# A fused adaLN, local-attention and gated-MLP kernel on one core: the opening's loads on two queues, another order of the work behind it, an edge constant built on GpSimd, and the gate row in column tiles

## The chip, the core and the metric

The kernel runs on one NeuronCore of a Trainium2 chip. A core has a matrix engine (TensorE, PE in the profile, with its weight loads shown apart as PEld), three engines for everything else (VectorE or DVE, ScalarE or ACT, GpSimd or POOL) and SyncE (SP), which issues transfers. Transfers issued by SP run on the queue q1 of the profile, those of GpSimd on q0, those of ScalarE on q10; all share the core's 16 DMA engines. The metric is the device time of one execution in microseconds. Three executions of the kernel before took 544.57, 543.80 and 543.88 us, median 543.88 us.

## The reference

One transformer block with 2048 rows and 576 columns, conditioned on one vector `c`.

```
mod = (silu(c) @ w_mod).reshape(1, 6, 1, 576)      # sa, ca, ga, sb, cb, gb
h = layernorm(x) * (1 + ca) + sa
q, k, v = h @ wqkv                                 # 32 heads of 18
logits[s, w] = q[s] . k[s - 2 w] * 18 ** -0.5      # w = 0..7, masked before row 0
x = x + ga * ((softmax(logits) @ v[s - 2 w]) @ wo)
h = layernorm(x) * (1 + cb) + sb
x = x + gb * (((h @ w_gate) * (h @ w_up)) @ w_down)   # 576 -> 4608 -> 576
```

Inputs and output are bfloat16. `sa`, `ca`, `sb`, `cb` act on columns of `h`, which stand on partitions in the kernel's transposed `h`. The two gates `ga` and `gb` act on rows of 576 columns and are therefore needed as one row repeated on all 128 partitions.

## The kernel before

The 2048 rows are eight chunks of 256 (`CH`), each of two tiles of 128 rows (`j` = 0, 1). The chunks go through attention one after the other and through the MLP in five groups, `[0], [1, 2], [3, 4], [5, 6], [7]`. The schedule is written out by hand: every engine does its instructions in the order of the program, a transfer is asked for by the engine that names it, and a later instruction of that engine waits behind it.

**Opening, 0 to 20 us.** SP asks for chunk 0 of x in two pieces (L203), the last 64 rows of the first two blocks of `w_mod` (`load_wm_tail`, two transfers, L190), the other 512 rows (L206), then `wqk`, chunk 1 of x, more of `wqk`, `wv` and `wmC` (the block of `ga`). ScalarE asks for `c` in three pieces into five partitions (L185, L187). PE turns `c` by one transpose (L1029); `keep_busy` (L199) gives it dummy matmuls meanwhile. `mod_columns` (L321 to L347) multiplies silu(c), repeated over 32 columns, with `wmA` in four column tiles at once, `k` order `KF, 0, 1, 2, 3`; the result is evicted to `mrow`, transposed, and added into `modc`. The normed chunk 0 is transposed in between (`x0_ts`) and evicted through `modc` to `hT`. Only then can the first matmul of q (L416) run. GpSimd meanwhile makes constants, among them `edge`.

**Middle, 20 to 48.8 us.** Chunk 0's attention by halves `j`: `pj` (products of q with a shifted k, DVE), `lj` (their head sums, PE), `max_j` and `sum_j` (softmax, DVE with an exponential on ACT), `shift_attn` (PE), `av_mul` (DVE), `av_sum` (PE), `b_wj` (the product with `wo`, PE, then the gated residual on DVE). Between them stand chunk 1's q, k, v (`a_q`, `a_v`) and chunk 2's norm. The first 16 rows of the second tile reach back into the first tile; they are corrected by `edge_mul` (DVE) and five matmuls with `edge_t`, which PE makes by seven matmuls from `edge` (L1143) and ACT copies. `mod_row` (L349) makes `ga` for all partitions: ten matmuls of full width with 512 and 64 columns, copied to `ga_bc`.

**Groups.** `gate_up` runs 36 steps `f`; each is a pair of 64-row matmuls for gate and up (L706). Four steps share one block of weights, 0.5 MB for gate and 0.5 MB for up, loaded by SP (`load_wgu`). Block 3 of group 0 has no buffer of its own: it stands in the tile `hh` (`wgu_home[3]`, L1319). Small pieces of other work stand between the steps. A planner (`timed`, L808) places them at build time: each piece is a tuple (PE cost, DVE cost, marks it needs, mark it sets, delay until that mark holds, call). In group 0 one thread of pieces loads the block of `gb` on GpSimd's queue (`load_wm5`) and, 12 planner units later, runs `gb_row` (L1257): `mod_row` for `gb`, then `ld_d1(3)`, a load of 576 KB of `w_down` on GpSimd's queue into a part of `hh` that nothing uses yet. Another thread is chunk 3's norm, made on ACT in two pieces of two instructions each (`norm_of`, L683).

Of the kernel before, what the change touches and what calls it, by code (L numbers as in the profile page):

```python
# [7 lines left out]
BF = mybir.dt.bfloat16  # L8
# [17 lines left out]
W = 8  # L26
# [12 lines left out]
VR = H - VA  # L39

# [4 lines left out]
def kernel(  # L45
# [31 lines left out]
    vstage = pool("vstage", 2)  # L77
# [25 lines left out]
    ga_bc = consts.tile([P, D], F32, name="ga_bc")  # L103
    gb_bc = consts.tile([P, D], F32, name="gb_bc")
# [10 lines left out]
    vd = dramp.tile([HALO + S, D], BF, name="vd")  # L115
    prod_t = consts.tile([P, 4 * KT * CH], BF, name="prod_t")
# [67 lines left out]
    c_row = sp.tile([KT, P], BF, name="c_row")  # L184
    nc.scalar.dma_start(c_row[0:KF, :], c[0, 0:KF * P].rearrange("(m p) -> m p", p=P))  # L185
    for c0 in (0, 64):
        nc.scalar.dma_start(c_row[KF:KT, c0:c0 + 64], c[:, KF * P:D])  # L187
    def load_wm_tail(wm, blk):
        for b in range(2):
            nc.sync.dma_start(wm[64 * b:64 * (b + 1), KF, b * D:(b + 1) * D], w_mod[KF * P:D, (blk + b) * D:(blk + b + 1) * D])  # L190
# [11 lines left out]
    for j in range(ST):  # L202
        nc.sync.dma_start(x_in[0][:, j, :], x_flat[js(j), :])  # L203
    load_wm_tail(wmA, 0)
# [23 lines left out]
    for k in range(2):  # L228
# [11 lines left out]
    edge = sp.tile([HALO, W - 1, P], BF, name="edge")  # L240
    edge_t = sp.tile([P, HALO], BF, name="edge_t")
# [3 lines left out]
    nc.gpsimd.affine_select(out=edge[:], in_=edge[:], compare_op=ALU.not_equal, fill=1.0, base=-2,  # L245
                            pattern=[[-(HALO + DIL), W - 1], [1, P]], channel_multiplier=-1)
    nc.gpsimd.affine_select(out=edge[:], in_=edge[:], compare_op=ALU.is_ge, fill=0.0, base=SPAN - 1,
                            pattern=[[-DIL, W - 1], [0, P]], channel_multiplier=-1)
    nc.gpsimd.memset(wo[64:, KF, :], 0.0)
# [10 lines left out]
    def ln_parts(src, tag, act=False, both=None):  # L260
# [22 lines left out]
        def norm_act(j):  # L283
            nb = small.tile([P, 1], F32, name="ln_nb")
            nc.vector.scalar_tensor_tensor(nb[:], mv[:, j, 0:1], -1.0, rstd[:, j:j + 1], ALU.mult, ALU.mult)
            for d0, s0, n in ((0, 0, D), (D, D - 64, 64))[0:2 if both else 1]:
                nc.scalar.activation(xn[:, j, d0:d0 + n], src(j)[:, s0:s0 + n], ACTF.Identity, bias=nb[:], scale=rstd[:, j:j + 1])
        return xn, stat, rsq, (norm, norm_act) if act is None else norm if not act else norm_act

    def layernorm(src, tag, act=False, both=None):  # L290
        xn, stat, rsq, norm = ln_parts(src, tag, act, both)
        for j in range(ST):
            stat(j)

        def norms(js=range(ST)):
            for j in js:
                norm(j)
        return xn, lambda: rsq(slice(0, ST)), norms
# [22 lines left out]
    def mod_columns(wm, pi, fill=lambda: None, steps={}):  # L321
        pm = ps([P, 320], F32, "pm")
        order = (KF, 0, 1, 2, 3)
# [25 lines left out]
    def mod_row(wm, dst):  # L349
        pa = ps([P, 512], F32, "pa")  # L350
        pb = ps([P, 64], F32, "pb")
        for p_t, c0, c1 in ((pa, 0, 512), (pb, 512, D)):
            for kt in range(KT):
                m = wm(kt)
                rows = slice(0, m.shape[0])
                nc.tensor.matmul(p_t[:], lhsT=sc_bc[rows, kt, :], rhs=m[:, c0:c1],
                                 start=(kt == 0), stop=(kt == KT - 1))
        nc.scalar.copy(dst[:, 0:512], pa[:])
        nc.scalar.copy(dst[:, 512:D], pb[:])
# [176 lines left out]
    def shift_attn(j):  # L536
# [6 lines left out]
        if j > 0:  # L543
            pzb = ps([P, H], F32, "pzb")
            for w in range(W - 1):
                nc.tensor.matmul(pzb[:], lhsT=edge[:, w, :], rhs=attn0[0:HALO, j, w, :], start=(w == 0), stop=(w == W - 2))
# [11 lines left out]
    def av_sum(j, hf, acc={}):  # L558
# [10 lines left out]
        if hf == 1:  # L569
            if j > 0:  # L570
                for d, c0 in dst:
                    nc.tensor.matmul(d[:, 0:HALO], lhsT=v_e[:].rearrange("p d h -> p (d h)")[:, c0:c0 + P], rhs=edge_t[:],
                                     start=False, stop=True, skip_group_check=True)
            nc.scalar.copy(oT[:, 0:KF, js(j)], po[:])
            nc.scalar.copy(oT[0:64, KF, js(j)], po4[64:P, :])

    def b_wj(j):
# [10 lines left out]
        def rest(stat):  # L588
            for hf, (cs, pw) in enumerate(pws):
                nc.vector.tensor_tensor(xt[:, cs], pw[:], ga_bc[:, cs], ALU.mult)  # L590
                nc.vector.tensor_tensor(xt[:, cs], xt[:, cs], x_res[0][:, j, cs], ALU.add)
                stat(j, (hf,))
        return rest
# [89 lines left out]
    def norm_of(n, after, free, load=None):  # L683
# [5 lines left out]
        norm = [(0, 0, f"r{n}", f"e{n}", 2.0, lambda: aa[n]["norm"]((0,))), (0, 0, f"e{n}", f"n{n}", 1.6, lambda: aa[n]["norm"]((1,)))]  # L689
# [325 lines left out]
    def load_wm5():  # L1015
        nc.gpsimd.dma_start(wm5(), w_mod[0:KF * P, 5 * D:6 * D].rearrange("(k p) n -> p k n", p=P))
# [11 lines left out]
    pc = ps([P, KT], BF, "pc")  # L1028
    nc.tensor.transpose(pc[:], c_row[:], ident[0:KT, 0:KT])  # L1029
    keep_busy(7, NB)  # L1030
# [25 lines left out]
    add_modc = mod_columns(wmA, 0, lambda: keep_busy(2, NB), {KF: x0_ts, 1: lambda: keep_busy(1, NB)})  # L1056
# [31 lines left out]
    ashs = {}  # L1088

    def sum_j(j):  # L1090
        ss = small.tile([P, H], F32, name="ssj")
        nc.vector.tensor_reduce(ss[:], dd0[:, j].rearrange("p w h -> p h w"), axis=AX.X, op=ALU.add)
        nc.vector.reciprocal(ss[:], ss[:])
        nc.vector.tensor_tensor(attn0[:, j], dd0[:, j], ss[:, None, :].to_broadcast([P, W, H]), ALU.mult)

    load_wm(wmC, 2, 1)
    for dd4 in range(4):
        nk = (DH - dd4 + 3) // 4
        wsrc = bass.AP(A_wo.tensor, A_wo.offset + dd4 * D, [[DH * D, H], [4 * D, nk], [1, D]])
        nc.sync.dma_start(wo[dd4 * H:(dd4 + 1) * H, 0:nk, :], wsrc)  # L1100
    load_res(0)
    load_wm_tail(wmB, 3)
    nc.sync.dma_start(wmB[:, 0:KF, :], w_mod[0:KF * P, 3 * D:5 * D].rearrange("(k p) n -> p k n", p=P))
    load_x(2)
# [36 lines left out]
    pet = ps([P, HALO], F32, "pet")  # L1141
    for w in range(W - 1):
        nc.tensor.matmul(pet[:], lhsT=edge[:, w, :], rhs=ident[0:HALO, 0:HALO], start=(w == 0), stop=(w == W - 2))  # L1143
    nc.scalar.copy(edge_t[:], pet[:])
    mod_row(lambda k: wmC[:, k, :], ga_bc)
    for w in range(4):
        lj(1, w)
    sum_j(0)
    a_q(1, 0)
    shift_attn(0)  # L1150
    for w in range(4, 8):
        pj(1, w)
    a_q(1, 1)
    for w in range(4, 8):
        lj(1, w)
    av_mul(0, 0)
    max_j(1)
    a_q(1, 2)
    av_mul(0, 1)
    sum_j(1)  # L1160
    a_q(1, 3)
    av_sum(0, 0)
    a_q(1, 4)
    av_sum(0, 1)
    shift_attn(1)
# [3 lines left out]
    xn2, stat2, rsq2, norm2 = ln_parts(lambda j: x1[0][j], "b")  # L1169
    stat2c(0)  # L1170
    stat2c(1)
    rsq2c(slice(0, 2))
    av_mul(1, 0)
    x1_halves = []

    def products_1():
        x1_halves.append(b_wj(0))
        norm2c(0)
        norm2c(1)
        a_v(1, 0)  # L1180

    add_modc = mod_columns(wmB, 1, products_1)
    x1_half = x1_halves[0]
    av_mul(1, 1)
    edge_mul()
    add_modc()
    av_sum(1, 0)
    x1_half(stat2)
    a_t(2, False)
    av_sum(1, 1)  # L1190
    b_p(1, 0)
    rsq2(slice(0, 1))
    a_v(1, 1)
# [17 lines left out]
    a_v(2, 0)  # L1211
    b_l(1, 0)
    for w in range(4, 8):
        b_p(1, w)
    a_v(2, 1)
# [41 lines left out]
    def gb_row():  # L1257
        mod_row(lambda k: wm5()[:, k, :] if k < KF else wm5r[0:64, :], gb_bc)
# [3 lines left out]
    first = [(0, 0, "", "p17", 1.4, nop), (0.75, 0, "p17", "l14", 1.0, lambda: b_l(1, 4)), (0.35, 0, "l14", "t14", 0.3, lambda: b_lt(1))] + first  # L1262
# [8 lines left out]
               [[(0, 0, "", "-", 0, lambda: (load_wm5(), load_wd(0))), (0, 0, "", "z3", 8.0, both_halves), (0, 0, "", "w5", 12.0, nop), (1.5, 0, "w5", "-", 0, gb_row), (0, 0, "", "-", 0, lambda: load_res(2))],  # L1271
# [3 lines left out]
                                         (0.6, 0.8, "n4 v3", "x4", 0, lambda: (a_t4(), load_x(6)))]]),  # L1275
# [84 lines left out]
```

## Time and profile before

| what | value |
|---|---|
| median of three runs | 543.88 us |
| the profiled execution's own time | 544.44 us |
| its span, first to last instruction | 542.7 us |
| PE busy | 535.3 us, 99% of the span |
| DVE busy, ACT busy | 58%, 46% |
| first matmul of q (L416) starts | 11.09 us |
| first matmul of gate and up (L706) starts | 48.83 us |
| DVE busy in 15 to 20, 20 to 25, 25 to 30, 30 to 35 us | 4.70, 4.81, 4.41, 4.55 of 5 us each |
| bytes moved in 48.8 to 64.6 us | 5.36 MB, 339 GB/s |
| granted TensorE clock | 1.0 |

The span is what the profile covers; the time of an execution has some 1.7 us around it. Windows of the span are given from its start. A chain of waits follows the work back from the last instruction: at each step to what released it. The DMA share is the mean busy share of the 16 engines; a little over 1 is a full engine, since records overlap.

### The profile page before, as it was taken

The page shows a single profiled execution, that of the slowest core. Times are in us where ns is not written, and L with a number is a line of the kernel's source. Part 1 is how long each engine was busy: PE and PEld are TensorE (multiplying, and loading weights), DVE is VectorE, ACT ScalarE, POOL GpSimd, SP SyncE. Part 2 cuts the span into 40 slices and gives each one's busy share as a digit, 9 for nine tenths or more (in the row PEclk, how much of TensorE's full clock was granted, in tenths as well). Part 3 has the DMA queues.
Part 4 walks back from the last instruction along what each step waited for, and adds up shares of the span by engine and source line. Part 5 has one row for each costly group of instructions (what it writes and reads, how often), then busy time and mean ns, then how long its engine had stood idle before and what let it go on. Part 6 is the DMA issues. An engine that isn't in the chain of part 4 may idle for free.

```text
span 542.7 us, 14569 instructions
## 1 busy us (share of the span) xinstructions
PE 535.3 (99%) x6157; PEld 321.9 (59%) x6189; DVE 315.9 (58%) x713; ACT 251.5 (46%) x617; POOL 67.9 (13%) x104
## 2 busy tenths in 40 slices
PE   8999999999999999999999999999999999999997
PEld 4887789756745444555544444555544445558875
DVE  4989586777766777646358896524344924032212
ACT  4776777543566553022645552014555551006630
POOL 7104012122000110111000110110010101010210
PEclk9999999999999999999999999999999999999999
DMA  8999999778872694878435983894296592849821
GB/s 264 299 261 363 336 272 332 258 224 258 267 203 89 211 208 153 227 220 293 135 108 163 232 288 68 162 239 159 89 275 176 156 311 69 255 138 294 271 74 42
DMA packets 94924, 114.52 MB, mean 211 GB/s; under 512 B 27980, under 2 KB 83676, under 8 KB 94732
## 3 DMA queue, kind: packets, MB, share of 16 engines
q1 hardware_dynamic: 83360, 67.29, 44.6%
q0 software_dynamic: 11344, 46.25, 27.8%
q8 instruction: 48, 0.79, 0.6%
q14 instruction: 16, 0.13, 0.1%
q10 hardware_dynamic: 156, 0.07, 0.0%
HBM read 103.15 MB, written 4.74 MB: 199 GB/s over the span
## 4 chain that ended last, share of the span: by engine, by line
PE 94%; DMA 3%; DVE 1%; SPq 1%; ACT 1%; issue 0%
PE pg L706 28%; PE pu L706 23%; PE acc L921 19%; PE pq L706 3%; PE accr L926 3%; PE pw L605 3%; PE pq L416 3%; PE acc L976 3%; PE lgT L470 2%; DMA wmC<-in_w_mod_dram 2%; PE pv L706 2%; PE pv L439 1%; DMA wqk<-in_A_wqkv_dram 1%; PE po L567 1%; PE pwj L584 0%
## 5 line engine op out<-in xcount | busy, mean ns | idle before, releaser
L706 PE MATMUL pg<-h2T,wgu 64*128 64x512 bf16 (+1 forms) x1376 | 265.5, 331 | 0.0
L706 PE MATMUL pu<-h2T,wgu 64*128 64x512 bf16 (+1 forms) x1376 | 264.5, 331 | 0.0
L706 PEld LDWEIGHTS <-wgu 64*128 64x128 bf16 x2752 | 136.5, 94 | 94.8 <-issue 0.5
L757 ACT CAST u_sb<-pu 128x512 bf16<-128x512 f32 (+1 forms) x172 | 85.4, 497 | 135.8 <-PE pg L706 131.2
L760 DVE TENSOR_TENSOR hh<-g_sb,u_sb 128x512 bf16<-128x512 bf16 x136 | 57.4, 423 | 116.2 <-ACT g_sb L758 115.7
L758 ACT CAST g_sb<-pg 128x512 bf16<-128x512 f32 (+1 forms) x172 | 86.7, 504 | 0.0
L921 PEld LDWEIGHTS <-hh 128*128 128x128 bf16 x504 | 49.0, 98 | 59.5 <-issue 1.5
L921 PE MATMUL acc<-wd,hh 128*128 128x512 bf16 x329 | 84.1, 380 | 0.1
L926 PE MATMUL accr<-wd,hh 128*128 128x64 bf16 x344 | 62.4, 193 | 0.7
L706 PE MATMUL pu<-h2T,wgr 64*128 64x512 bf16 (+1 forms) x188 | 61.5, 327 | 0.2 <-ACT u_sb L757 0.2
L706 PE MATMUL pg<-h2T,wgr 64*128 64x512 bf16 (+1 forms) x188 | 61.5, 327 | 0.0
L926 PEld LDWEIGHTS <-hh 128*128 128x128 bf16 x504 | 45.8, 98 | 1.9
L171 POOL DMA_DIRECT2D wd<-in_B_w_down_dram x29 | 21.8, 752 | 190.0 <-PE accr L926 93.4
L461 DVE TENSOR_TENSOR prod_t<-qT,kT 128x1280 bf16<-128x1280 bf16 x56 | 43.7, 818 | 0.7 <-ACT kT L777 0.7
L514 DVE TENSOR_TENSOR vsh<-vsh,attn 128x1152 bf16<-128x1152 bf16 x56 | 39.6, 748 | 1.2 <-DMA vsh<-vd 1.2
L706 PEld LDWEIGHTS <-wgr 64*128 64x128 bf16 x376 | 19.7, 94 | 15.4 <-issue 2.5
L921 PE MATMUL acc<-prod_t,hh 128*128 128x512 bf16 x111 | 28.8, 380 | 0.0
L304 ACT ACTIVATE h2T<-h2T,modc 128x256 bf16<-128x256 bf16 x12 | 6.6, 595 | 45.3 <-DMA h2T<-xn 45.3
L455 POOL DMA_DIRECT2D vsh<-vd x14 | 12.5, 897 | 104.8 <-DVE o_sb L524 89.6
L706 PE MATMUL pq<-hT,wqk 64*128 64x256 bf16 (+1 forms) x360 | 22.2, 259 | 0.1
L416 PE MATMUL pq<-hT,wqk 128*128 128x256 bf16 (+1 forms) x225 | 21.2, 251 | 0.4 <-ACT hT L304 0.4
L926 PE MATMUL accr<-prod_t,hh 128*128 128x64 bf16 x112 | 21.6, 193 | 0.1
(208 smaller groups left out, 605.0 us busy)
## 6 DMA issues: line engine op xcount, KB each, us to landing
wgu<-in_B_w_gate_dram SPq DMA_DIRECT2D x41, 512.0 KB, 4.5
wgu<-in_B_w_up_dram SPq DMA_DIRECT2D x41, 512.0 KB, 6.4
wd<-in_B_w_down_dram POOLq DMA_DIRECT2D x29, 576.0 KB, 5.6
vsh<-vd POOLq DMA_DIRECT2D x14, 1152.0 KB, 9.3
prod_t<-in_B_w_down_dram POOLq DMA_DIRECT2D x8, 576.0 KB, 7.6
hh<-in_B_w_down_dram POOLq DMA_DIRECT2D x6, 576.0 KB, 6.4
x_r<-in_A_x_dram SPq DMA_DIRECT2D x8, 288.0 KB, 8.3
vd<-v_sb POOLq DMA_DIRECT2D x16, 144.0 KB, 5.2
```

The lines of the kernel that those rows point to most:

```text
L171: return nc.gpsimd.dma_start(wb[:], B_w_down[r0:r0 + FB * P, :].rearrange("(k p) n -> p k n", p=P))
L416: nc.tensor.matmul(pq[:, gi, :], lhsT=wqk[:, kt, m * P:(m + 1) * P], rhs=hT[:, kt, cols], start=(kt == order[0] and not (by_k and gi)), st ...
L461: nc.vector.tensor_tensor(prod, aa[i]["qT"][:], aa[i]["kT"][:, :, off:off + CH], ALU.mult)
L514: nc.vector.tensor_tensor(v, v, at, ALU.mult)
L605: nc.tensor.matmul(pw[:], lhsT=oT[:, m, js(j)], rhs=wo[:, m, 0:512], start=(m == 0), stop=(m == KT - 1))
L706: return nc.tensor.matmul(out, lhsT=lhs, rhs=rhs, start=first, stop=last, skip_group_check=True)
L757: nc.scalar.copy(u[:, c, :], pu)
L758: nc.scalar.copy(g[:, c, :], pg)
L760: return lambda: nc.vector.tensor_tensor(hh[:, f - c:f + 1, :], g, u, ALU.mult)
L921: nc.tensor.matmul(acc[j][:], lhsT=hh[:, f, js(j)], rhs=wb[:, f % FB, 0:512], start=(f == 0), stop=(f == FT - 1))
L926: nc.tensor.matmul(accr[:, j, :], lhsT=hh[:, f, js(j)], rhs=wb[:, f % FB, 512:D], start=(f == 0 and j == 0), stop=(f == FT - 1), skip_grou ...
L976: nc.tensor.matmul(acc[i][:], lhsT=hh[:, f, js(j)], rhs=wb(f)[:, c0:c1], start=(f == 0), stop=(f == FT - 1))
```

## The change

The diff, cut to its core. Opening:

```diff
-    c_row = sp.tile([KT, P], BF, name="c_row")
-    nc.scalar.dma_start(c_row[0:KF, :], c[0, 0:KF * P].rearrange("(m p) -> m p", p=P))
-    for c0 in (0, 64):
-        nc.scalar.dma_start(c_row[KF:KT, c0:c0 + 64], c[:, KF * P:D])
+    c_row = sp.tile([1, D], BF, name="c_row")
+    nc.scalar.dma_start(c_row[:], c[:, :])
...
-    for j in range(ST):
-        nc.sync.dma_start(x_in[0][:, j, :], x_flat[js(j), :])
-    load_wm_tail(wmA, 0)
+    nc.sync.dma_start(x_in[0][:], x_rows(0))
+    load_wm_tail(wmA, 0, nc.scalar)
...
-    pc = ps([P, KT], BF, "pc")
-    nc.tensor.transpose(pc[:], c_row[:], ident[0:KT, 0:KT])
-    keep_busy(7, NB)
+    pc = ps([P, KT], F32, "pc")
+    for r0, r1, m, c0 in [(0, P, m, m * P) for m in range(KF)] + [(0, 64, KF, KF * P), (64, P, KF, KF * P)]:
+        nc.tensor.matmul(pc[r0:r1, m:m + 1], lhsT=c_row[:, c0:c0 + r1 - r0], rhs=ident[0:1, 0:1], start=True, stop=True, skip_group_check=True)
+    keep_busy(6, NB)
...
-    add_modc = mod_columns(wmA, 0, lambda: keep_busy(2, NB), {KF: x0_ts, 1: lambda: keep_busy(1, NB)})
+    x0_ts()
+    add_modc = mod_columns(wmA, 0, lambda: keep_busy(2, NB), {KF: lambda: keep_busy(1, NB)}, (0, 1, KF, 2, 3))
```

Edge constant (`edge` is now zero-padded to 128 partitions, and its reader L546 uses all of them), and the softmax's division:

```diff
+    nc.gpsimd.memset(edge_t[:], 0.0)
+    for w in range(W - 1):
+        d = edge_t[:, 0:SPAN - DIL * w]
+        nc.gpsimd.affine_select(out=d, in_=d, compare_op=ALU.not_equal, fill=1.0, base=-DIL - (HALO + DIL) * w,
+                                pattern=[[-1, SPAN - DIL * w]], channel_multiplier=1)
...
-        nc.vector.reciprocal(ss[:], ss[:])
-        nc.vector.tensor_tensor(attn0[:, j], dd0[:, j], ss[:, None, :].to_broadcast([P, W, H]), ALU.mult)
+        nc.scalar.activation(ss[:], ss[:], ACTF.Ln)
+        nc.scalar.activation(ss[:], ss[:], ACTF.Exp, scale=-1.0)
+        sums[j] = ss
+
+    def share_j(j):
+        nc.vector.tensor_tensor(attn0[:, j], dd0[:, j], sums.pop(j)[:, None, :].to_broadcast([P, W, H]), ALU.mult)
```

The middle's order. In SP's queue chunk 2 of x is asked for ahead of `x_r` and the second `wmB`; `vstage` has four buffers instead of two; `edge_mul` stands between the two halves of `b_wj`'s residual; `av_out` is the end of `av_sum` (the edge's matmuls and the copies to `oT`) as a function of its own. From `pj(1, 3)` on the order is

```
before: edge_t on PE; ga; lj(1,0..3); sum_j(0); a_q(1,0); shift_attn(0); pj(1,4..7); a_q(1,1);
  lj(1,4..7); av_mul(0,0); max_j(1); a_q(1,2); av_mul(0,1); sum_j(1); a_q(1,3); av_sum(0,0);
  a_q(1,4); av_sum(0,1); shift_attn(1); stat2c; rsq2c; av_mul(1,0); mod_columns(wmB) with
  b_wj(0), norm2c, a_v(1,0) in it; av_mul(1,1); edge_mul; add_modc; av_sum(1,0); x1 half; a_t(2);
  av_sum(1,1) with its end; b_p(1,0); rsq2; a_v(1,1); ...
after: a_q(1,0); ga; sum_j(0); lj(1,0..3); pj(1,4..5); share_j(0); a_q(1,1); shift_attn(0);
  pj(1,6..7); a_q(1,2); lj(1,4..7); max_j(1); av_mul(0,0); a_v(1,0); sum_j(1); av_mul(0,1);
  a_q(1,3); av_sum(0,0); share_j(1); a_q(1,4); shift_attn(1); stat2c(0); av_sum(0,1); stat2c(1);
  mod_columns(wmB) with b_wj(0) in it; av_mul(1,0); rsq2c; norm2c(0); av_mul(1,1); norm2c(1);
  av_sum(1,0); av_sum(1,1); x1 half with edge_mul in it; transposes of chunk 2; av_out(1);
  their evictions; rsq2; b_p(1,0); a_v(1,1); add_modc; ...
```

and after that `a_v(2, 1)` stands ahead of `b_l(1, 0)`. The gate row, with `GC = D // 4`, both gate rows in bfloat16 instead of float32, and the planner:

```diff
+    def gb_cols(wm):
+        pa = ps([P, GC], F32, "pa")
+        for kt in range(KT):
+            for q in range(4):
+                nc.tensor.matmul(pa[H * q:H * (q + 1), :], lhsT=sc_bc[:, kt, 0:H], rhs=wm(kt)[:, GC * q:GC * (q + 1)],
+                                 start=(kt == 0), stop=(kt == KT - 1), skip_group_check=True)
+        grow = wm5r[:, 0:GC]
+        nc.scalar.copy(grow, pa[:])
+        nc.gpsimd.dma_start(gd[:], grow[0:P:H, :])
+        nc.gpsimd.dma_start(gb_bc[:], bass.AP(gd.tensor, gd.offset, [[0, P], [1, D]]))
...
     def load_wm5():
+        nc.gpsimd.memset(wm5r[64:, :], 0.0)
...
     def gb_row():
-        mod_row(lambda k: wm5()[:, k, :] if k < KF else wm5r[0:64, :], gb_bc)
+        gb_cols(lambda k: wm5()[:, k, :] if k < KF else wm5r[:])
         ld_d1(3)
...
-    first = [(0, 0, "", "p17", 1.4, nop),
+    first = [(0, 0, "", "p17", 2.2, nop),
...
-  (1.5, 0, "w5", "-", 0, gb_row)
+  (0.85, 0, "w5", "-", 0, gb_row)
...
-  (0.6, 0.8, "n4 v3", "x4", 0, lambda: (a_t4(), load_x(6)))
+  (0.6, 0, "n4 v3", "x4", 0, lambda: (a_t4(), load_x(6)))
...
-        norm = [(0, 0, f"r{n}", f"e{n}", 2.0, lambda: aa[n]["norm"]((0,))), (0, 0, f"e{n}", f"n{n}", 1.6, lambda: aa[n]["norm"]((1,)))]
+        norm = [(0, 0, f"r{n}" if k == 0 else f"e{n}{k - 1}", f"e{n}{k}" if k < 3 else f"n{n}", 1.0 if k < 3 else 1.6, lambda k=k: aa[n]["norm"]((k // 2,), (k % 2,)))
+                for k in range(4)]
```

`gd` is a small tensor in DRAM; chunk 3's norm on ACT becomes four pieces of one instruction each.

## The prediction

> **What bounds the kernel now.** I read the page first, then the chain of waits in order of time, then the transfers in short windows, then the few places where PE stood still.
>
> ```profile
> span 542.7 us, 14569 instructions
> ...
> PE 535.3 (99%) x6157; PEld 321.9 (59%) x6189; DVE 315.9 (58%) x713; ACT 251.5 (46%) x617; POOL 67.9 (13%) x104
> ...
> PE 94%; DMA 3%; DVE 1%; SPq 1%; ACT 1%; issue 0%
> ```
>
> PE is busy for 99% of the span and holds 94% of the chain. So only two things can shorten the kernel: PE's real work starting earlier, or PE having less to do. The chain's ends of DMA and its PE pieces show where:
>
> ```profile
> 4.11 6.48 DMA wqk<-in_A_wqkv_dram
> ...
> 11.76 8.89 DMA wmC<-in_w_mod_dram
> 20.65 0.14 issue
> 20.79 0.38 PE pa L356
> ...
> 62.77 0.32 PE pa L356
> 63.09 0.05 issue
> 63.15 0.91 PE pa L356 x3
> 64.06 0.36 PE pb L356 x5
> 64.42 0.09 PE pu L706
> 64.50 0.13 PE pg L706 x2
> 64.64 0.28 PE pu L706
> ```
>
> Two transfers end waits of PE (10.59 and 20.65 us), and the gate row `gb` stands on PE from 62.77 to 64.42 us. Less plain is the last line: right behind the row, the up weights of block 3 (tile `hh`) are used at 64.64 us. They had been asked for at 41.67 us and took 22.9 us, so they landed at 64.57 us; PE waited some 0.2 us (steps are 0.11 us apart, here it was 0.27).
>
> ```profile
> hh<-in_B_w_up_dram SPq DMA_DIRECT2D x1, 512.0 KB, 22.9
> ...
> hh<-in_B_w_down_dram POOLq DMA_DIRECT2D x1, 576.0 KB, 12.4
> ```
>
> (DMA issues; the last column is us from issue to landing.) The second line is `ld_d1(3)`, issued by GpSimd at 52.86 us, landed at 65.26:
>
> ```profile
> 52.86 0.76 POOL L171 DMA_DIRECT2D hh<-in_B_w_down_dram  x1
> 79.17 0.75 POOL L171 DMA_DIRECT2D wd<-in_B_w_down_dram  x1 [25.55 <-DMA lg_t<-lgs]
> ```
>
> In 48.8 to 64.6 us GpSimd's queue moved 3.84 MB and SP's 1.49 MB:
>
> ```profile
> q0 software_dynamic: 960, 3.84, 72.4%
> q1 hardware_dynamic: 1592, 1.49, 32.0%
> ```
>
> So up to block 3 there are two bounds, nearly level: PE's work, and a stream of transfers that has kept the DMA engines full since about 5.5 us. Whatever PE gains before 64.4 us counts only if that stream gains as much. Before 5.5 us the stream is not full (columns: PE busy and count, clock, DMA share, GB/s):
>
> ```profile
> 3.00:3.50 0.50, 0.50 (x3) 1.00 0.58 143
> 4.50:5.00 0.50, 0.50 (x3) 1.00 0.69 106
> 6.50:7.00 0.50, 0.50 (x3) 1.00 1.05 410
> ```
>
> **The change, part by part, on PE.**
>
> *Opening.* The first q matmul, 11.09 us, waits for `hT` (0.43 us), behind `modc`, `mrow`, and the last `mod_columns` matmuls, which ran from 8.88 to 9.33 us as the main part of `wmA` landed. SP now spends one issue on x instead of two (0.87 to some 0.45 us, from a single load's 0.39 to 0.61) and none on the tails (1.19 us, now on ScalarE's queue), so `wmA` is asked for at about 1.3 instead of 2.97 us. With weights early, x decides: its first half landed at 2.99 and its second, asked for at 1.28 and taking 2.3, near 3.5; as one request I take 3.45 (3.2 to 4.1). The first norm's halves, ready at 6.30 and 6.15, move to about 6.75. Then on PE: ten transposes 0.65, the first two `k` 0.45, the tail 0.2, one dummy 0.22, the last two 0.45: end at 8.7 instead of 9.33. Gain 0.6 us (0 to 0.9). ACT's queue now issues the tails (1.15 us for 0.53 of two small `c` loads), so its table load (1.28 us) ends near 3.85 instead of 3.24, still ahead of its first use, about 4.5. Six one-row matmuls for `c` against one transpose (0.18 us) replace one dummy matmul; if this cover were gone they cost at most six times 0.18.
>
> *Middle.* The seven edge matmuls and the wait for `wmC` fill 20.30 to 20.79 us, and both go: `a_q(1, 0)`, 1.1 us, now covers the landing of `wmC`. GpSimd pays with a memset and seven small selections, about 1 us by 0.31 us for one of 156 columns as a ceiling of each; they lie behind its constants near 11 us, and what they delay, the copy into `sc_bc` (11.51), is read at 20.8. DVE loses two reciprocals (0.35 us each); ACT gains four small instructions (0.2 to 0.27). Laying out the new order with the old durations from 20.3 us: `max_j(1)` now stands ahead of `av_mul(0, 0)`, so DVE idles some 1.2 us until the last `lj(1, ..)` at 25.65; then `av_mul(0, 0)` ends at 27.95 against PE's need at 28.0, `share_j(1)` at 30.27 against 30.25, `av_mul(1, 0)` at 33.75 against 34.55. PE then reaches `a_q(2, 0)` with no wait over 0.1 us. DVE had two idle stretches of 0.7 us (for x of chunk 2, for `v_e`) which the new order fills. Gain 0.3 us (bounds: the whole 0.49; a loss of 1.2, if DVE's idle reaches PE).
>
> *Chunk 3's norm.* Two ACT instructions in a row (1.20 us) held `u_sb` back: PE's steps of 0.11 us have one of 0.45 there.
>
> ```profile
> 58.90 0.27 PE L706 MATMUL pu<-h2T,wgr 64*128 64x256 bf16 x1 [0.18 <-ACT u_sb L757]
> ```
>
> One at a time they fit: gain 0.3 us (0 to 0.34).
>
> *Gate row.* Ten wide matmuls, 1.65 us of chain, become 20 column-tile matmuls of 144 columns. The nearest rows: 20 of 256 columns take 0.66 us (L470), 20 of 320 take 0.90 (L328), 20 of 32 columns 0.49 (L1076, full width). I take 0.5 (0.45 to 0.9). Gain 1.15 us (0.75 to 1.2). ACT copies 144 columns instead of 576. The trip through DRAM stands on GpSimd's queue, nothing else of which is due before 79.17 us; `gb_bc` is first read after 98 us.
>
> *bfloat16 gates.* Their DVE products read PSUM and take 0.44 us for 288 columns; the residual's addition without PSUM takes 0.31. I take no change; if the bfloat16 operand brought them to the addition's speed, the tail's last three products (0.69, 0.42, 0.42) would lose up to 0.4 us.
>
> Planner pieces that move by a step change no PE work. On PE before block 3: 0.6 + 0.3 + 0.3 + 1.15 = 2.35 us. PE would want the up weights at 64.47 - 2.35 = 62.1 us.
>
> **And on the transfers.** *Start.* From 2 to 6 us 0.81 MB moved (the eight half-us windows). At x's 250 GB/s to 3.2 us and then 400, it would be 1.4 MB, 1.5 us earlier at 395 GB/s; the earlier request bounds it at 1.65. I take 1.3 us (0.4 to 1.65). *Relief.* `ld_d1(3)` used to be issued at 52.86 us, waiting for nothing. In the new program GpSimd's queue first holds the two `gd` transfers, and the first waits for ACT's copy of the row, near 61 us; so those 576 KB leave the stream ahead of block 3. The load ahead of it on q0 landed at 63.17, so until 64.57 about two thirds of it had been moved, 0.35 MB: at 0.34 MB/us 1.0 us (0 to 1.2). The up weights land at 64.57 - 2.3 = 62.3 us, 0.15 after PE wants them. The gain at block 3 is then 2.3 us, and both bounds share it. Later, block 4 (landed 68.07, used 68.4) has the same relief, and block 5 (landed 70.9, used 74.3) has 3.4 us, of which the displaced load, 1.7 us at 0.34 MB/us, can take half. If that cover were gone, 1.7 us come back.
>
> [...]
>
> **The sum.** 542.7 - 2.3 = 540.4 us of span. The profiled execution took 544.44 and the median is 543.88; I put the gain on the median: 541.6 us. Own range 540.8 to 542.4.
>
> **The rivals.**
> 1. *Transfers bind at block 3* (14%): the displaced load brings nothing there, because GpSimd's larger share of bandwidth is used by its own earlier `vsh` loads instead. For it: 3.84 against 1.49 MB. Against: total bytes ahead of block 3 do fall. Gain 1.3: 542.6.
> 2. *x comes late* (10%): the tails' 147 KB at 250 GB/s lie ahead of x's end, landing near 4.1; the opening gains nothing, the rest 1.7: 542.2. Against: the tails are asked for after x.
> 3. *Given back* (11%): the displaced load and the gate's trip meet block 5 and chunk 3's transposes (5.2 us to landing), which a DVE wait of 1.4 us for `hT` shows already late; PE waits 1.7 + 0.7 us around 70 us. 543.9, no change.
> 4. *Slower* (15%): the middle turns DVE-bound. DVE was busy 4.4 to 4.8 of each 5 us from 15 to 35 us, and each share now waits for two ACT instructions in ACT's own order, with `max_j(1)` blocking `av_mul(0, 0)` behind it. If the four hand-overs to PE (two shares, `av_sum(0, 0)`, `av_out(1)`) each cost 0.9 us, 3.6 are lost and 1.3 net: 545.2. It decides from 2.3 us lost on; against it stands the layout above, which loses 0.1.
>
> **Chances.** The forecast has 50%. Within 0.2% (1.1 us, about what a measurement can tell from no change) lie the third rival and some of the first: 15%. Faster has the rest of the first, the second, and the forecast: 70%. Slower 15%. The range runs from 540.6 (every PE term at its better end: 0.9 + 0.49 + 0.34 + 1.2 and the wait's 0.2 give 3.1, a little more with the tail) to 544.0, which takes in all but the slower case.
>
> **What would show it.** The first q matmul near 10.5 us; the first gate matmul near 47.9 (48.83 before); the gate row under 0.6 us; no L171 load on GpSimd between 52 and 62 us; `hh` up weights landing near 62.3. I am wrong if the middle, from the first q matmul to the first gate matmul (37.74 us before), grows, if `ld_d1(3)` still goes out at 53 us, or if PE waits at block 3 or 5.

## The result, and the profile after

The changed kernel took 550.76 us (median of six executions, 547.77 to 554.67), the kernel before on the same chip 543.87 (543.59 to 544.57). The ratio is 1.0133, 95% interval 1.0104 to 1.0161: 6.9 us slower by the medians and 7.2 by the ratio, where 541.6 and a gain had been forecast. The profiled execution took 551.04 us.

The page of the changed kernel (span, busy time by engine, shares of the chain):

```profile
span 549.3 us, 14595 instructions
...
PE 534.5 (97%) x6165; PEld 319.4 (58%) x6196; DVE 315.1 (57%) x711; ACT 251.1 (46%) x619; POOL 71.1 (13%) x115
...
PE 93%; DVE 2%; DMA 2%; ACT 1%; issue 1%
```

PE did no more work than before (534.5 against 535.3 us), but the span is 6.6 us longer: PE stood still. The waits of PE between 50 and 100 us say where (us in total, times, longest):

```profile
PE pv L734 <- issue: 4.9, 1, 4.9
PE pu L734 <- DVE ln_nb L294: 0.9, 1, 0.9
PE pa L371 <- DMA hh<-in_w_mod_dram: 0.4, 1, 0.4
```

The chain in order of time gives their places, and those of the forecast's marks:

```profile
0.82 2.94 DMA x_t<-in_A_x_dram
...
11.05 5.19 PE pq L433 x90
...
56.06 6.63 DMA hh<-in_w_mod_dram
62.83 0.50 PE pa L371 x20
...
85.60 3.47 issue
89.07 0.99 PE pv L734 x10
```

The gate row takes 0.50 us, as forecast. But in front of it the chain hangs for 6.63 us on the weights of that row (`wm5`), of which PE itself stood 0.4 us, and at 85.60 us it waits for nothing that the profile shows. Windows around that place (PE busy and count, clock, DMA share, GB/s):

```profile
78.00:80.00 2.00, 2.00 (x47) 1.00 1.59 364
80.00:82.00 2.00, 2.00 (x37) 1.00 1.60 193
82.00:84.00 2.00, 2.00 (x40) 1.00 0.46 54
84.00:86.00 2.00, 0.17 (x3) 1.00 0.69 206
86.00:88.00 2.00, 0.00 (x0) 1.00 1.07 341
88.00:90.00 2.00, 0.93 (x12) 0.88 1.04 341
90.00:92.00 2.00, 2.00 (x22) 0.50 0.82 279
92.00:94.00 2.00, 2.00 (x30) 0.77 0.42 140
```

From 80 us on the transfers nearly stop, to 54 GB/s at 82 to 84 us, though 1.77 MB of down weights are on order; this stretch is called the jam below. The kernel before had full transfers there. Its lowest window from 70 to 90 us is at 74 us, beside the second of two DMA transposes on SP's queue that turn the logits (`lgs` to `lg_t`, asked for at 73.67 us), and PE did not stand for it:

```profile
74.00:76.00 2.00, 2.00 (x42) 1.00 0.61 163
...
82.00:84.00 2.00, 2.00 (x40) 1.00 1.05 369
```

PE stops at 84.18 in the changed kernel, and after 4.9 us of standing it runs at a granted clock of 0.5 for about 3.4 us: 22 matmuls in 2 us instead of 40. Last, GpSimd's requests (start, duration, what; in brackets the idle time before):

```profile
49.77 0.57 POOL L1044 MEMSET o_t<- 64x576 bf16 x1
56.06 0.76 POOL L1045 DMA_DIRECT2D hh<-in_w_mod_dram  x1 [5.72 <-PE pg L734]
...
64.47 0.61 POOL L375 DMA_DIRECT2D gd<-o_t  x1 [6.31 <-ACT lgs L490]
71.12 0.57 POOL L376 DMA_DIRECT2D gb_bc<-gd  x1 [6.04 <-DMA gd<-o_t]
71.69 0.78 POOL L174 DMA_DIRECT2D hh<-in_B_w_down_dram  x1
75.33 0.76 POOL L174 DMA_DIRECT2D wd<-in_B_w_down_dram  x1 [2.86 <-DMA lg_t<-lgs]
```

The second line was this in the kernel before:

```profile
50.77 0.76 POOL L1016 DMA_DIRECT2D hh<-in_w_mod_dram  x1 [0.45 <-DVE prod_t L461]
```

So `wm5` is asked for 5.3 us later, `ld_d1(3)` (the line at 71.69) 18.8 us later, and the next down weights, `wd(1)`, 3.8 us earlier. The row's trip through DRAM is 7.2 of the 18.8 us: its second transfer waited 6.04 us for its first to land, and the load stands behind both.

### The profile page after: what moved, and what is told of

The parts are those of the page before. It is cut to its first block, busy times and chain, and to the rows that moved or that the text cites. A ratio compares the mean times of both kernels' runs of the same rounds, so it can differ in the third digit from the quotient of the medians.

```text
span 549.3 us, 14595 instructions
## 1 busy us (share of the span) xinstructions
PE 534.5 (97%) x6165; PEld 319.4 (58%) x6196; DVE 315.1 (57%) x711; ACT 251.1 (46%) x619; POOL 71.1 (13%) x115
## 4 chain that ended last, share of the span: by engine, by line
PE 93%; DVE 2%; DMA 2%; ACT 1%; issue 1%
PE pg L734 27%; PE pu L734 22%; PE acc L949 19%; PE pq L433 4%; PE accr L954 3%; PE pw L632 3%; PE acc L1004 3%; PE pq L734 2%; PE pv L734 2%; PE pv L456 2%; PE lgT L487 2%; DMA hh<-in_w_mod_dram 1%; PE po L587 1%; DVE ln_statsa L276 1%; DMA x_t<-in_A_x_dram 1%
## 5 line engine op out<-in xcount | busy, mean ns | idle before, releaser
L734 PEld LDWEIGHTS <-wgu 64*128 64x128 bf16 x2752 | 134.5, 94 | 96.5 <-issue 0.4
L734 PEld LDWEIGHTS <-wgr 64*128 64x128 bf16 x376 | 18.6, 94 | 17.2 <-issue 3.2
```

The source lines that it names most:

```text
L734: return nc.tensor.matmul(out, lhsT=lhs, rhs=rhs, start=first, stop=last, skip_group_check=True)
```

## The experiments

Three theories were tried. Theory F: GpSimd's instructions come in blocks by DMA (the traces list packets of 8 KB, kind `instruction`, on a queue q14), and the added ones move a block's end to just in front of the request for `wm5`. Theory J: the down weights of 75 us jam the transfers. Rival M: the order, or the row's trip through DRAM with the displaced load. Medians, with the kernel before measured beside each, and the ratio with its 95% interval (e17 is e9's kernel again, e18 is e15's):

| kernel | us | before | ratio |
|---|---|---|---|
| e1_before_pad15 | 545.77 | 544.05 | 1.0038 (1.0025 to 1.0052) |
| e2_after_pad16 | 550.16 | 544.05 | 1.0123 (1.0092 to 1.0155) |
| e3_wd_behind7 | 546.62 | 544.05 | 1.0040 (1.0028 to 1.0052) |
| e4_pad_wd7 | 544.28 | 544.05 | 1.0002 (0.9990 to 1.0015) |
| e5_gate_only | 545.49 | 544.45 | 1.0017 (1.0003 to 1.0031) |
| e6_x_two | 544.43 | 544.45 | 1.0006 (0.9994 to 1.0017) |
| e7_norm_back | 544.91 | 544.45 | 1.0012 (1.0000 to 1.0023) |
| e8_open_only | 544.22 | 544.45 | 0.9993 (0.9979 to 1.0006) |
| e9_p17_back | 543.56 | 544.31 | 0.9984 (0.9973 to 0.9996) |
| e10_row_back | 546.28 | 544.31 | 1.0039 (1.0024 to 1.0054) |
| e11_d13_first | 544.98 | 544.31 | 1.0014 (1.0000 to 1.0028) |
| e12_open_gate | 543.45 | 544.31 | 0.9990 (0.9975 to 1.0004) |
| e13_after_d13_first | 545.60 | 543.79 | 1.0040 (1.0022 to 1.0059) |
| e14_middle_only | 544.29 | 543.79 | 1.0007 (0.9996 to 1.0017) |
| e15_p17_norm | 543.99 | 543.79 | 1.0000 (0.9989 to 1.0010) |
| e16_pad_d13_p17 | 544.22 | 544.34 | 0.9999 (0.9983 to 1.0015) |
| e17_split_again | 543.75 | 544.34 | 0.9991 (0.9980 to 1.0003) |
| e18_nosplit_again | 543.40 | 544.34 | 0.9989 (0.9974 to 1.0004) |

Marks of PE and GpSimd in the profiled executions (us; q: first q matmul, gate: first gate or up matmul, row: its first matmul, down: first matmul of the down product). Each row is one execution; that of e4, 545.73 us, was the slowest of its ten:

| kernel | q | gate | wm5 asked | row | wd(1) asked | down |
|---|---|---|---|---|---|---|
| before | 11.09 | 48.83 | 50.77 | 62.71 | 79.17 | 98.11 |
| after | 11.05 | 48.20 | 56.06 | 62.83 | 75.33 | 103.87 |
| e1 | 11.22 | 48.77 | 56.29 | 64.27 | 78.94 | 98.97 |
| e2 | 10.96 | 48.20 | 50.21 | 62.32 | 76.35 | 102.49 |
| e4 | 11.06 | 49.70 | 51.80 | 63.82 | 86.40 | 98.66 |
| e10 | 10.93 | 48.08 | 55.86 | 63.05 | 77.34 | 99.15 |
| e12 | 10.96 | 48.51 | 50.56 | 62.38 | 77.92 | 96.70 |
| e13 | 11.04 | 48.31 | 56.33 | 62.91 | 76.95 | 97.69 |
| e18 | 10.90 | 48.05 | 50.15 | 62.47 | 81.97 | 96.62 |

**The late request.** e1 is the kernel before and e2 the changed kernel, each with this, 15 and 16 times:

```diff
     nc.gpsimd.tensor_copy(sc_bc[:, :, H:], ...)
+    pad = sp.tile([P, 16], BF, name="pad")
+    for _ in range(15):
+        nc.gpsimd.memset(pad[:], 0.0)
```

> The kernel before with fifteen tiny GpSimd memsets (128x16) behind its copy into sc_bc; nothing else, and nothing reads them. Theory F (GpSimd's own instruction stream is fetched in blocks by a DMA of 8 KB, and the change's added GpSimd instructions move the end of a block to just in front of the request for wm5): the request (L1016 + the new lines), at 50.77 us before, goes out 3 to 6 us later, with an 8 KB packet just ahead of it, the gate row starts 1 to 4 us later, and the median grows by 0.5 to 3 us. Rival M (the late request comes from the new order of the work, from a semaphore that the change made late): the request stays at 50.8 us and the time at 543.9 +- 0.5.

Fifteen memsets that nothing reads, done before 18 us, moved a request at 50 us. GpSimd in e1:

```profile
56.29 0.76 POOL L1016 DMA_DIRECT2D hh<-in_w_mod_dram  x1 [6.03 <-PE pu L706]
```

Among the queues of e1 from 53 to 56 us stands what came in between; no such packet lies there in the kernel before:

```profile
q14 instruction: 1, 0.01, 0.8%
```

The request went out 5.5 us later: theory F holds, and rival M falls for this part. In e1 PE then waits 1.6 us for `wm5`, and the median grows by 1.7.

> The changed kernel with sixteen tiny GpSimd memsets behind its copy into sc_bc, where GpSimd is idle. Theory F: the block's end falls among the memsets near 15 us, the request for wm5 goes out at 50.5 instead of 56.06 us, wm5 lands near 57, the gate row stands where the planner put it and PE waits for nothing there: the span loses 0.5 to 1.5 us by that alone, and more if the jam of 80 to 86 us (PE still for 4.9 us) hung on the late request: down to 543. Rival M: the request stays at 56 us, the time at 547.8 to 554.7. Rival J (the jam comes from the loads of the down weights against the DMA transposes and not from wm5): the request moves, the 4.9 us stall at 84 us stays, 549 to 550.

The request went out at 50.21 us, and no wait for `wm5` is left. But 550.16: the late request is not the main loss. The jam stayed, in another form:

```profile
PE pg L734 <- DMA wgu<-in_B_w_gate_dram: 1.7, 1, 1.7
PE busy L201 <- DVE busy_w L196: 1.3, 1, 1.3
PE pu L734 <- DMA wgu<-in_B_w_up_dram: 1.2, 1, 1.2
```

Here PE lacked weights, not instructions: the up weights asked for at 79.20 us took 16.55. PE then ran at half clock for 3.4 us again, from 96.6 us. (The second line is there in every kernel.)

**The jam.** `behind` holds a load until another has landed. e3 is the changed kernel with this line, e4 has the sixteen memsets too:

```diff
-    loads = {(0, 20): lambda: behind(load_wd(1), wgu_in[6]), ...
+    loads = {(0, 20): lambda: behind(load_wd(1), wgu_in[7]), ...
```

> The changed kernel with the three loads of down weights on GpSimd's queue (wd 1, d1 4, wd 2) held behind the up weights of block 7 instead of block 6, so that they go out at 86 instead of 75.33 us. Theory J (these 1.77 MB on GpSimd's queue, met by the second DMA transpose of lgs, jam the DMA engines from 80 to 86 us; PE's own instruction block of 16 KB, due near 81 us, comes at 86.5 and PE stands still from 84.18 to 89.07): the transposes are over by 80 us, PE's block comes near 81.5, the stall of 4.9 us and the clock of 0.5 behind it go, and the median falls by 4 to 7 us, to 544 to 547. Rival M (the gate row's trip and the displaced load d1 3 are the cause): the jam stays or moves and the time stays near 550.

> Both edits of the two kernels before together: sixteen memsets, and the down weights behind block 7. Theories F and J together: the request for wm5 at 50.5 us, no stall at 84 us; what is left of the change is its gain: 541 to 543 us. If the prediction's own rivals hold (x late, given back) 543 to 544. Rival M: above 546.

e3 came near the upper end of what theory J gave, e4 just above what the forecast's own rivals gave, 543 to 544. The stall and the low clock are gone from both. e2 to e4 is 5.9 us for the hold, e3 to e4 2.3 us for the memsets; without the hold the memsets brought 0.6 us (550.76 to 550.16), less than either kernel's own spread. How long a load of down weights takes from its issue says it in one line; this is the changed kernel, 72 to 80 us (two issues, KB each, median us to landing):

```profile
wd<-in_B_w_down_dram POOLq DMA_DIRECT2D x2, 576.0 KB, 15.2
```

and this is e13 below, with loads of the same size issued 1.6 us later:

```profile
wd<-in_B_w_down_dram POOLq DMA_DIRECT2D x2, 576.0 KB, 7.6
```

**Which part makes the jam.** e5 has the new row alone on the kernel before, e10 the changed kernel with the old row (both by the lines of the change's own diff for `gb_cols`, `gd`, `load_wm5` and the 0.85). e13 moves one line of the changed kernel, e11 the same line in e4:

```diff
     def gb_row():
+        ld_d1(3)
         gb_cols(lambda k: wm5()[:, k, :] if k < KF else wm5r[:])
-        ld_d1(3)
```

> The kernel before with the gate row alone in its new form (20 column-tile matmuls, its trip through DRAM, the load d1 3 behind it, the planner's 0.85); opening, middle and chunk 3's norm as before. The prediction's own terms: the row 1.65 to 0.5 us, 1.15 us of gain, shared by both bounds because d1 3 leaves the stream: 542.7. Rival M (the trip and the displaced load cause the loss): the jam of 80 to 86 us is here too, PE stands still for 2 to 5 us near 84, 545 to 549. Theory J in its wide form (the jam needs both the earlier stream of the new opening and the displaced load): 542.7 to 543.5, and no stall.

> The changed kernel with the gate row as it was (ten wide matmuls, copies of 512 and 64 columns, no trip through DRAM, the load d1 3 asked for with wm5, the planner's 1.5); the gate constant stays bfloat16, and there are no memsets and no other hold. Rival M (the displaced load and the gate's trip are needed for the jam): no stall of PE at 84 us, the clock stays at 1, 545 to 546.5 (the late request for wm5 and the wide row stay). Theory J (the jam is the down weights against the second transpose of lgs, and comes from the new order of what goes before): PE stands still for 3 to 5 us, 549 to 552.

> The changed kernel with one edit: d1 3 is asked for ahead of the gate row's two transfers on GpSimd's queue, so that it goes out right behind wd 0 near 58 us instead of 71.69. No memsets, no hold. If the displaced load makes the jam (its 576 KB meet the up weights and the second transpose of lgs at 72 to 80 us): the down weights go out at 77 us or later, no stall at 84 us, clock 1, 545 to 546.3. If the shorter row and its trip make it: the stall of 3 to 5 us stays, 548.5 to 552.

> The changed kernel with the sixteen memsets and the down weights behind block 7 (544.28 measured), and d1 3 asked for ahead of the gate row's two transfers on GpSimd's queue instead of behind them, so that it goes out near 53 us as before. If the displaced load is what takes the row's gain back between 65 and 98 us (from the end of the row to the first down matmul the kernels with the new row took 34.3 to 34.5 us, those with the old one 33.0 to 33.7): that stretch falls to 33.0 to 33.7 and the time to 543.3 to 543.8. If the relief counts as the prediction had it: block 3's up weights land 1 us later and the time rises to 544.5 to 545. If the planner's pieces set the stretch: no change, 544.0 to 544.5.

e10's trace has no stall, so the new row has a part in it. e13 keeps the new row and only asks for the load early: 545.60, and in its profile the transfers run through the place where they stood before:

```profile
80.00:82.00 2.00, 2.00 (x41) 1.00 1.03 341
82.00:84.00 2.00, 2.00 (x41) 1.00 1.04 356
84.00:86.00 2.00, 1.90 (x30) 1.00 1.01 332
```

The trip through DRAM is still there, so this points to the displaced 576 KB: in e13 they are asked for at 58.43 us and in at 67.0; in the changed kernel they are on the way from 71.69 to 78.3, and three more loads of 576 KB join them at 75.33. Four of e13's twelve executions still took 547.1 to 549.5, which suggests that the early load makes the jam rare, not impossible; those executions have no trace, but their granted clock, 0.995 to 0.998 against 1.0 in the traced one, would fit a stall with half clock behind it. e13's down weights also went out 0.6 us later than e2's, so what the load's place does by itself and what it does through that is not separated. e5, the row alone, has no stall of that kind either, with the displaced load at 71.80 and `wd(1)` at 80.62 us: its time lies where rival M put it, its trace where the wide theory J did. In its profile it lost where a late `v_e` held DVE 1.5 us near 37 and late up weights PE 1.1 us near 93, and came out slower than before, against the 542.7 of the forecast's terms. With the hold in place (e11) the early load brought nothing: 544.98 lies in the range that was given for a loss by it. From the end of the row (63.08 us) to the first down matmul (97.93) it still took 34.9.

Why the down weights went out early is read from the traces, not tried. `wd(1)` is held behind block 6's up weights, and these had moved ahead of the first transpose of `lgs` in SP's queue. The changed kernel, then the kernel before:

```profile
67.25 0.88 SPq L157 DMA_DIRECT2D wgu<-in_B_w_up_dram  x1
68.22 2.20 SPq L504 DMA_TRANSPOSE lg_t<-lgs  x1
```

```profile
70.27 1.18 SPq L487 DMA_TRANSPOSE lg_t<-lgs  x1
71.54 0.53 SPq L154 DMA_DIRECT2D wgu<-in_B_w_gate_dram  x1
72.13 0.49 SPq L154 DMA_DIRECT2D wgu<-in_B_w_up_dram  x1
```

All kernels here with the planner's p17 at 2.2 have the first order, all with 1.4 the second. Without the hold, `wd(1)` goes out at 75.3 to 77.3 us in the traces of the former and at 77.6 to 80.6 in those of the latter (the opening alone, e8: 77.6). So p17 may have a share in the jam; no run has the changed kernel with p17 alone put back.

**The opening.** e8 is the opening alone on the kernel before, e6 is e4 with x in two requests:

```diff
-    nc.sync.dma_start(x_in[0][:], x_rows(0))
+    for j in range(ST):
+        nc.sync.dma_start(x_in[0][:, j, :], x_flat[js(j), :])
```

> The kernel before with the new opening alone (x in one request, the weight tails on ScalarE's queue, c as one row with six small matmuls, x's transposes ahead of the modulation columns and the order 0, 1, tail, 2, 3); all else as before. Prediction: first q matmul 10.5 instead of 11.09 and a stream 1.3 us earlier: 543.2. Theory X: first q matmul within 0.1 us of 11.09, the stream up to 9 us earlier at block 3, the time 543.7 to 544.1, and no stall. Rival J-wide (the earlier stream alone sends the down weights into the DMA transposes): the three loads go out 2 to 4 us earlier than 79.17, PE stands still near 84 us, 545 to 549.

> The changed kernel with the sixteen memsets and the down weights behind block 7 (544.28 measured), and x of chunk 0 again as two requests on SP's queue instead of one; the tails stay on ScalarE's queue. Theory X (x as one request lands at 3.8 instead of 2.99 us for its first half, and this alone ate the opening's gain): the first statistics start near 3.0, x's transposes end 0.4 to 0.7 us earlier, the first q matmul comes near 10.6 instead of 11.05, 543.7 to 543.9. Rival (the weights bind, or the tails on ScalarE's queue slow x whatever its shape): the first q matmul stays within 0.15 us of 11.05, 544.3.

Theory X falls: the first q matmul came at 11.30 us, not near 10.6. The weights are what the chain of e6 waits for:

```profile
2.21 6.85 DMA wmA<-in_w_mod_dram
...
11.30 0.22 PE pq L434
```

With x in two requests `wmA`, asked for at 2.21 us and landed at 9.06, ends last; in the changed kernel it was x, landed at 3.76 us. e8's first q matmul came at 11.45; there PE waited for the tails, which ScalarE asked for at 1.94 us and which landed at 8.64 (6.70 us; 5.5 in the changed kernel, and on SP's queue in the kernel before some 2.4). No opening tried here was clearly earlier than 11.0.

**The wait for ln_nb.** DVE in the changed kernel: the second tile's `ln_nb` stands behind the softmax's two operations, ScalarE's norm waits for it, and the evictions that PE needs stand behind that norm.

```profile
59.77 0.68 DVE L511 TENSOR_REDUCE mx<-lg 128x64 f32<-128x512 bf16 x1
60.48 0.69 DVE L512 TENSOR_TENSOR dd<-lg,mx 128x512 f32<-128x512 bf16 x1
61.09 0.15 DVE L294 SCALAR_TENSOR_TENSOR ln_nb<-ln_mva,ln_rstda 128x1 f32<-128x1 f32 x1
```

e7 takes the split of the norm back in e4, e9 only the planner's delay:

```diff
-    first = [(0, 0, "", "p17", 2.2, nop), ...
+    first = [(0, 0, "", "p17", 1.4, nop), ...
```

> The changed kernel with the sixteen memsets and the down weights behind block 7 (544.28 measured), and chunk 3's norm in two planner pieces of two ScalarE instructions as before instead of four of one. Theory N (in the new split the second tile's small DVE instruction ln_nb is asked for in a piece that stands behind DVE's reduction and subtraction of another chunk, 1.4 us, and ScalarE's in-order queue holds PE's copies behind it: PE waits 0.9 us near 62 us): the wait goes, 543.4 to 543.7. Rival (the wait comes from where the planner puts the softmax pieces, whatever the split): PE waits as long there or at a neighbouring place, 544.1 to 544.6.

> The changed kernel with the sixteen memsets and the down weights behind block 7 (544.28 measured), and the planner's delay in front of chunk 3's work (p17) at 1.4 us as before instead of 2.2. Theory P (the longer delay moves chunk 3's norm behind the softmax's reduction and subtraction on DVE, 1.4 us, so that ScalarE's in-order queue stops at the norm and PE waits 0.9 us near 62 us; undoing the split did not help): ln_nb of the second tile comes ahead of the reduction again, the wait of 0.9 us goes, 543.3 to 543.7. Rival (it comes from the new order of the middle, which leaves the chunk later against the gate blocks): the wait stays, 544.0 to 544.6.

In e7 the 0.9 us stayed; in e9 they went, and the ratio fell to 0.9984 with an interval that excludes 1; e17, the same kernel, gave 0.9991 with one that takes in 1. DVE in e9, in the other order:

```profile
59.02 0.15 DVE L294 SCALAR_TENSOR_TENSOR ln_nb<-ln_mva,ln_rstda 128x1 f32<-128x1 f32 x1
...
60.63 0.68 DVE L511 TENSOR_REDUCE mx<-lg 128x64 f32<-128x512 bf16 x1
```

**Single terms, and what is best.** e12 is the opening and the row with `ld_d1(3)` early, e14 the middle alone (with sixteen memsets), e15 and e18 are e9 without the split, e17 is e9 again, e16 is the changed kernel with the memsets, `ld_d1(3)` early and p17 at 1.4.

> The kernel before with the new opening and the new gate row, d1 3 asked for ahead of the row's trip; middle, edge constant, planner's p17 and chunk 3's norm as before. No GpSimd block's end falls in front of a load that is due, and the down weights go out as before. If the row's 1.1 us and the opening's 0.2 add up: 542.8 to 543.2, better than both. If the gain is given back at the weights of later blocks whatever the queue's order: 543.8 to 544.3.

> The kernel before with the new middle alone (the order from 20 to 39 us, the edge constant on GpSimd, the reciprocals as two ScalarE instructions, x of chunk 2 asked for earlier, bfloat16 gate constants), sixteen memsets on GpSimd so that no block's end falls in front of wm5; opening, gate row, chunk 3's norm and all planner values as before. The prediction's term: 0.3 us of gain at the first gate matmul (48.83 before, 48.5 here), 543.9 to 544.1 against 544.3 of the kernel before on these chips. The prediction's fourth rival (DVE-bound, 1 us and more lost): first gate matmul after 49.8, 545.3. Theory V (the middle gains some 0.6 us in executions where the load of v_e lands in time, by 36 us, and loses up to 0.8 where it does not): the time 543.8 to 544.5 with a wider spread than the kernel before.

> The kernel that was measured at 543.56 (the changed one with sixteen memsets, the down weights behind block 7 and the planner's p17 at 1.4 us), and chunk 3's norm in two pieces of two ScalarE instructions as before. The prediction's term (the split gives 0.3 us, 0 to 0.34): 543.8 to 543.9. If the split gives nothing once the delay is right: 543.4 to 543.7. If the split itself costs (it puts the two tiles' norms 1 us further apart): 543.0 to 543.3.

> The changed kernel with three edits: the sixteen memsets, d1 3 ahead of the gate row's transfers, the planner's p17 at 1.4 us; the down weights stay behind block 6. If the late wm5, the displaced load and the delay are the three causes of the loss: 542.5 to 543.5, faster than the kernel before, and no PE wait over 0.5 us behind 11 us. If the displaced load is a cause only by chance of timing (e13 had executions at 547 to 549.5 among its twelve): the median 543.5 to 545 with single executions above 547.

> The kernel that was measured at 543.56 once more, beside its twin without the split. If the split of chunk 3's norm gives the forecast's 0.3 us: 0.2 to 0.4 us below the twin. If it gives nothing: within 0.2 us of it.

> The twin: chunk 3's norm in two pieces of two ScalarE instructions. If the split gives the forecast's 0.3 us: 0.2 to 0.4 us above the kernel with it. If the wait that the split brings in the profile (0.3 us on lgT, 0.5 us on up weights) eats its gain: level with it or below.

e12's 543.45 lies between its two ranges and decides neither. The middle alone: its first gate matmul came 37.16 us after the first q matmul (37.74 before), but the time was no different from before. The split: e15's 1.0000 against e9's 0.9984 looked like a gain, but side by side the same two kernels, e17 and e18, came out the other way round, 543.75 and 543.40; it is worth nothing that can be measured. e16 came level with before, above the 542.5 to 543.5 expected for the three causes, with one execution at 546.7. The best of all are e9 (and e17, the same kernel), e12 and e18, 0.6 to 0.9 us under the kernel before; their intervals overlap, only e9's own excludes 1, and e18's kernel had come out level with before as e15. All have the new opening and gate row and none of the three losses; two of the three have the new middle as well, which fits with its showing nothing alone.

## Why the prediction was wrong, point by point

- **Gate row, 1.65 to 0.5 us: right.** 0.50 us measured.
- **"Nothing else of which is due before 79.17 us", and block 5's "1.7 us come back": this is the step that failed.** The relief was worked out up to block 3 and came (its up weights landed at 55.0 us, not 62.3; already 59.3 with the opening alone, e8, so the start was sized too small). The displaced load was then priced as one transfer against block 5's slack, with no term for the row's trip ahead of it (7.2 us). So it went out at 71.69 us, past block 5, and met the loads of blocks 6 and 7, the second transpose of `lgs` and three down-weight loads that were themselves let go 3.8 us earlier. That cost 5 to 6 us (e2 to e4; the changed kernel's ratio against e3's), not 1.7. The third rival named the load and sized it at a third of that. None of the prediction's three signs of being wrong came: the middle shrank, `ld_d1(3)` went out late, and PE waited for weights at neither block 3 nor block 5.
- **Edge constant on GpSimd, "what they delay, the copy into `sc_bc`": wrong in kind.** The seven selections took 1.76 us, inside the ceiling though above the 1 us taken, and delayed nothing that was read. But they are instructions: with them the request for `wm5` went from 50.77 to 56.06 us (55.86 in e10, which has them without the memset of `wm5r`), which theory F puts down to a block's end in front of it. Such a late request cost 1.7 us alone (e1), 2.3 in the changed kernel with the hold (e3 to e4), 0.6 without it.
- **"Planner pieces that move by a step change no PE work": true, and beside the point.** p17's 0.8 us more set chunk 3's norm behind a softmax: 0.7 us in the medians of e4 and e9, 1.0 in their ratios (0.6 with e17's), and a wait of 0.9 us in the traces. It also goes with the early down weights, as said above.
- **Opening, 0.6 us: 0.04.** The second rival's place, and half its reason: x as one load landed at 3.76 us, 0.3 later than taken, and the changed kernel's chain runs through it; yet in e6 and e8 the weights end last (`wmA` and the tails).
- **Middle, 0.3 us: 0.6 in its own stretch** (11.05 to 48.20; 0.4 against e8 and e12, which have the old middle), none of which e14 could show at the end. The fourth rival did not happen in the changed kernel's profile; in e4 it did for another reason, a `v_e` load of 12.2 us that held PE 1.1 us at 38 us.
- **Split of chunk 3's norm, 0.3 us: nothing** (e17 and e18).
- **Two slips that change nothing.** The transfer that landed at 10.59 us ended a wait of SP's queue, not of PE. Two thirds of `ld_d1(3)` are 0.39 MB rather than 0.35.

The three losses add to 8 or 9 us (5 to 6, 2, 1), a little more than was lost, and as the memsets show they do not simply add. Without them the change is worth at most 0.9 us rather than 2.3 (e9, e15 to e18: from 0.2 us above the kernel before to 0.9 under it). Of the forecast's gain the opening and the split are missing by measurement; that the middle's 0.6 us do not arrive at the end is measured (e14), not explained.

Why the engines move so little from 80 to 84 us stays open. In the traces the jam stands only where the displaced load and the early down weights meet, and taking away either takes it away; e13's four slow executions warn that the first may not be strictly needed. No run moves the transpose by itself. That PE then lacked its own next instructions is read from one trace (below), not tried by itself.

## What to carry to other kernels

Where the transfers are nearly full for long, a load that is moved must be followed to its new place and set against everything queued there, and so must every load that the relief lets go earlier. An instruction added to an engine that is idle can cost more than its time: here fifteen small memsets moved a request from 50.77 to 56.29 us and the median by 1.7 us (e1), so after such an edit look for a request that went out late with nothing to wait for. A planner's delay sets an order of instructions (here 0.8 us more put `ln_nb` behind 1.4 us of softmax, and PE waited 0.9 us): look at what now stands ahead of each small operation that another engine waits for.

## What the runs showed of the hardware that was not expected

The traces list packets of a kind `instruction` beside those of the data. Over the whole span of the changed kernel:

```profile
q8 instruction: 48, 0.79, 0.6%
...
q14 instruction: 17, 0.14, 0.1%
```

Here some came late by microseconds. One on q14, 8 KB, read here as a block of GpSimd's instructions, started 3.8 us after the end of GpSimd's last instruction in front of it (50.3 to 54.1 us), and GpSimd stood 5.7 us; in e2, with the memsets, no such packet lies between 53 and 56 us. Those on q8 have 16 KB and are read as PE's. In the kernel before three of them start at 73.10, 81.19 and 87.76 us, in the changed kernel at 74.30, 86.41 and 92.48. From 86 to 88 us of the changed kernel, right behind the stop at 84.18 us and ahead of the restart at 89.07, this line is there, and none from 76 to 86:

```profile
q8 instruction: 1, 0.02, 3.4%
```

In the packet records of that trace the packet on q14 ends at 54.51 us and GpSimd's next instruction follows 1.55 us later; the one on q8 ends at 87.49, and PE restarts 1.58 us later. The equal delay speaks for the same cause on both engines, and so for the reading that PE's 4.9 us were a wait for its own instructions.

From 80 to 84 us of the changed kernel 0.49 MB moved, and GpSimd's queue held nearly all the packet time with 99 packets:

```profile
q0 software_dynamic: 99, 0.42, 96.5%
q1 hardware_dynamic: 98, 0.06, 5.1%
```

That is 0.62 us a packet of GpSimd's queue, as an estimate from the share; the same working on the line of the prediction for 48.8 to 64.6 us gives 0.19, and on e2 from 82 to 84 us (20 packets, 40.5%) 0.65. In the packet records of the changed kernel from 80 to 84 us 13 of the 99 took more than 1 us, the longest 6.02, and the median was 0.20; in the kernel before the longest of 227 in the same stretch took 0.75. So some of the packets were slow, besides being few.

After 4.9 us of standing PE ran at half its clock from 89.5 to 92.9 us (0.50 granted at 90 to 92 us, 1.00 from 94 us on), so that a stall of 4.9 us cost, as an estimate, some 6.6 (half of 3.4 more). In e2, where PE was busy for 2.8 of the 6 us from 90 to 96, the clock was 0.64 at 96 to 98 us, 0.50 at 98 to 100 and 1.00 at 100 to 102.
